# Other instruction times in a source-level scheduler, and a place reserved by Gram, in a delta-rule and SoLU kernel

## The chip, the cores and the metric

The kernel runs on one core of a Trainium2 chip. The metric is device time of one execution in microseconds (us); the median of several executions is given, and one execution has also been recorded by the hardware profiler.

## What is computed

First a delta-rule attention over 768 steps, for 4 batches and 8 heads of width 48, then a SoLU layer with layer norm on the 3072 rows of width 384 that come out.

```python
def _attn_ref(q, k, v, beta):
    k_n = k / (np.linalg.norm(k, axis=-1, keepdims=True) + 1e-06)
    state = zeros((B, H, D, D))
    for t in range(S):
        y[:, :, t] = q[:, :, t] @ state            # per batch and head
        v_old = state^T k_n[:, :, t]
        state += beta[:, :, t] * outer(k_n[:, :, t], v[:, :, t] - v_old)

def _moe_ref(x, w_in, w_out, g_ln):
    h = x @ w_in                                   # 384 -> 1024
    solu = h * softmax(h)
    ln = (solu - mean(solu)) / sqrt(var(solu) + 1e-06) * g_ln
    return ln @ w_out                              # 1024 -> 384
```

## The kernel before

**Tiling.** The 768 steps are cut into 12 chunks of 64. A unit is one chunk of one pair of batches (`bp`), with its 8 heads, so there are 24 units. Inside a chunk the recurrence is replaced by a triangular system. Its matrix is inverted for a whole group `m` of units at once: group 0 and group 6 hold two units, groups 1 to 5 four each (`units`, line 437).

**The steps of a unit.** `gram` (line 498) multiplies the keys with themselves (`gram`) and with the queries (`qk`), 16 pairs of products into two places of the PSUM pool `ps_f`; ScalarE copies the first to `g`, which SP stores to DRAM, and VectorE masks the second into `pm`, the tile that the text calls P, in a pool of ten places (line 503). `begin` (lines 806 to 812) loads the stored Grams of a group across partitions (`to_inv`), and prepares the matrix. `inversion` (line 799) runs 30 steps of two vector operations, `itmp` and `y`: on GpSimd (POOL) from group 2 on, shared between VectorE (DVE) and GpSimd for groups 0 and 1 (line 564). `inv_end` (line 577) stores the inverse (`zd`, `xd`) and loads it back transposed, in runs of 128 bytes, into `zt`, `gx` and `gy`. `tlevel` (line 639, in `block_level`) puts the blocks of the inverse together with small products (`mps`), which need both places of `ps_f`. `chain` (line 649) carries the state from unit to unit (`kps`, `ups`, `cps`, `yps`) and ends with two transposing DMAs of the unit's rows. `moe_h` (line 709) is the first layer (`h`, 18 products in one PSUM buffer), the softmax and the row sums on VectorE and ScalarE, and two more transposing DMAs; `moe_out` (line 759) is the second layer (`ops`, 24 products) and the store. At the start the weights arrive as 64-bit floats and `to_f32` (line 377) takes them apart with three bit operations on VectorE; the result is split in a high and a low fp16 part.

**What sets the order.** The source does not issue instructions as it runs. `Engine` and `Queue` wrap the engines and hand each call to a `Recorder` (line 117) with a duration in ns (`occ`) and a latency. `Engine` reckons `base + per * n` for n elements of a partition, with 150 + 1.04 n on VectorE, 110 + 0.96 n on ScalarE, 200 + 1.8 n on GpSimd and hand-set numbers for products (218 per product of the first layer, 165 of the second); a call with `accum_out` gets 190 more (line 282). `Queue` reckons 5 ns per KB of a DMA as time of the single queue SP, and 2000 ns more until the data are there (line 295). Each call also carries a rank (`prio`), which comes from its stream: unit i's chain is due at i - 1, its first layer at i + 1.15, its second at i + 2.5, the Grams of group m at 4m - 11 and later, its inversion from about 4m - 6.8 on (lines 832 to 854).

`Recorder.order` (line 178) then simulates the engines. Whenever one is free, it takes, of the calls whose inputs are there by its clock, the one with the lowest rank. A call that is the first to use a tile of a pool with few places can only go when a place is free, and is put back if not (lines 217 to 231). Products within `rec.atomic()` form one call. The result is one list of all calls in the order of their simulated starts. `emit` issues that list, and on the chip each engine runs its part of the list in order, waiting at each instruction for the semaphores of its inputs. The simulated times themselves are not used on the chip, only the order is.

`hold` (line 161) notes a use of a tile by the call added last, without an operand in the instruction. `order` then treats the tile as in use from that call on.

Of the kernel before, what the change touches and what calls it, by code (L numbers as in the profile page):

```python
# [11 lines left out]
ALU = mybir.AluOpType  # L12
# [4 lines left out]
P = 128  # L17
# [250 lines left out]
class Engine:  # L268


    def __init__(self, rec, name, real, base, per, lat):
        self.rec, self.name, self.engine, self.base, self.per, self.lat = rec, name, real, base, per, lat

    def __getattr__(self, op):
        fn = getattr(self.engine, op)

        def call(*args, n=None, ns=None, slack=0, **kw):
            if ns is None:
                if n is None:
                    v = kw["in_"] if op == "tensor_reduce" else kw["out"] if "out" in kw else args[0]  # L280
                    n = v.count()
                ns = self.base + self.per * n + (190 if "accum_out" in kw else 0)
            return self.rec.add(self.name, fn, args, kw, ns, self.lat, slack)

        return call


class Queue:
# [5 lines left out]
    def dma_start(self, kb, **kw):  # L294
        return self.rec.add(self.name, self.engine.dma_start, (), kw, kb * 5.0, 2000)

    def transpose(self, kb, **kw):
        return self.rec.add(self.name, self.engine.dma_start_transpose, (), kw, kb * 5.0, 2000)
# [7 lines left out]
def kernel(  # L306
# [26 lines left out]
    pe = Engine(rec, "PE", nc.tensor, 0, 0, 200)  # L333
# [43 lines left out]
    def to_f32(u, raw, scale, n, nm):  # L377
        if raw.dtype == F32:
            dve.tensor_scalar(out=u, in0=raw[:, :n], scalar1=scale, scalar2=None, op0=ALU.mult)
            return  # L380
        w = raw.bitcast(I32)
        lo, hi = w[:, 0 : 2 * n : 2], w[:, 1 : 2 * n : 2]
        c = p2.tile([P, 512], F32, tag="wc", name=f"wc_{nm}")[:, :n]
        act.activation(c, hi.bitcast(F32), AF.Square)
        gps.tensor_scalar(out=c, in0=c, scalar1=(1.125 * 2.0**-15) ** 2, scalar2=scale, op0=ALU.is_ge, op1=ALU.mult)
        f = u
        u = u.bitcast(I32)
        dve.tensor_scalar(out=u, in0=hi, scalar1=3, scalar2=0x3FFFFFF8, op0=ALU.logical_shift_left, op1=ALU.bitwise_and)
        dve.scalar_tensor_tensor(out=u, in0=lo, scalar=29, in1=u, op0=ALU.logical_shift_right, op1=ALU.bitwise_or)
        dve.scalar_tensor_tensor(out=u, in0=hi, scalar=-(1 << 30), in1=u, op0=ALU.bitwise_and, op1=ALU.bitwise_or)  # L390
        gps.tensor_tensor(out=f, in0=f, in1=c, op=ALU.mult)
# [106 lines left out]
    def gram(m, u, t0):  # L498
# [10 lines left out]
        for h2 in range(0, H, 2):  # L509
            with rec.atomic():  # L510
                for h, b2 in hb[2 * h2 : 2 * h2 + 4]:
# [7 lines left out]
                    )  # L519
        rec.after = None  # L520
# [11 lines left out]
    def to_inv(m):  # L532
        gi = p2.tile([P, 32, 32], F32, tag="ginv", name=f"ginv_{m}")
        ginv[m] = gi
        for b in range(4):
            blk = b % 2
            for z in range(1 if len(units(m)) == 4 else 2):
# [4 lines left out]
                    kb=128, out=gi[32 * b + 16 * z : 32 * b + 16 * z + n],  # L542
# [18 lines left out]
    def inv_step(m, j):  # L561
# [3 lines left out]
        for eng, c0, c1 in parts:  # L565
            if c1 <= c0:
# [8 lines left out]
            eng.tensor_tensor(out=y[:, c0:c1, j + 1 : 32], in0=y[:, c0:c1, j + 1 : 32], in1=tv, op=ALU.add)  # L575

    def inv_end(m):
# [13 lines left out]
        for b in range(4):  # L591
# [3 lines left out]
            sp.dma_start(kb=128, out=zz[rows, 0:n, blk * 32 : blk * 32 + 32], in_=zd[r0 : r0 + n].rearrange("l j i -> j l i"))  # L595
            if blk == 0:
                for t, r1 in ((xx, r0), (xy, r0 + 32)):
                    sp.dma_start(kb=128, out=t[r1 : r1 + 32, 0:n], in_=xd[r0 : r0 + n].rearrange("l j i -> j l i"))
            else:
                sp.dma_start(kb=128, out=xx[rows, 0:n], in_=src[rows, 0:n, 0:32])  # L600
# [108 lines left out]
    def moe_h(ch, bp, t0):  # L709
# [31 lines left out]
        dve.scalar_tensor_tensor(out=pl, in0=pr, scalar=sc, in1=ph, op0=ALU.mult, op1=ALU.subtract)  # L741
# [187 lines left out]
```

## Time and profile before

| | |
|---|---|
| median of 3 executions | 515.21 us (514.75 to 515.44) |
| the profiled execution | 512.04 us |
| its span, first to last instruction | 510.2 us |
| TensorE, matrix products | 368.2 us busy, 72% |
| VectorE | 318.6 us, 62% |
| GpSimd (POOL) | 294.0 us, 58% |
| ScalarE | 192.9 us, 38% |
| transfers of the queue SP | 70.8% of 16 DMA engines |
| granted clock of TensorE, mean | 0.92 |

Times in rows of the profile are microseconds from the start of the span unless marked ns. PE is TensorE, PEld its weight loads, DVE VectorE, ACT ScalarE, SP the engine that issues the DMAs. A group of instructions is named by the tile that it writes and those that it reads (`h<-win_hi,xth`), with shapes, count, busy time and the mean of one. All instructions bear line 265, since `emit` issues them all. What stands behind `<-` at the end of a row is what ended the idle time before the instruction. Products overlap, so their mean times add up to more than they take.

### The profile page before, as it was taken

Reading aid. Unit: us, or ns where it says so; the run is one execution under the profiler, and the core shown is the slowest. Engines: PE = TensorE matmul, PEld = TensorE weight load, DVE = VectorE, ACT = ScalarE, POOL = GpSimd, SP = SyncE. Lnnn points to the kernel's source line nnn. Section 1 sums busy time; section 2 is a strip of 40 time slices with the busy share of each in tenths; the row PEclk is TensorE's granted clock in tenths of the full one; section 3 lists DMA queues with packets and bytes.
Section 4 is the critical chain, followed back from the end, with each engine's and each line's share of the span. In section 5 each row is a group of like instructions: output and inputs, shape, how many; then the busy total and the mean of one; then the engine's idle time right before and its main releaser. Section 6 shows DMA issues by size and latency. Waiting matters only on the chain.

```text
span 510.2 us, 18246 instructions
## 1 busy us (share of the span) xinstructions
PE 368.2 (72%) x7744; PEld 233.9 (46%) x7744; DVE 318.6 (62%) x791; ACT 192.9 (38%) x382; POOL 294.0 (58%) x506
## 2 busy tenths in 40 slices
PE   3510070689579488997598997787969797899974
PEld 3410070455346345665366564444635464566532
DVE  3599999887884383655088664256597355455670
ACT  2210241465522143536144544224345345454450
POOL 3378385966558998984016886008989898100000
PEclk9999999877876699998799998898989899999998
DMA  8685662987989949977999587985656866744332
GB/s 212 159 255 98 155 169 65 161 171 174 172 162 165 179 113 160 168 135 161 189 165 144 145 162 151 160 162 95 107 118 144 145 114 128 131 64 99 73 68 61
DMA packets 180640, 72.21 MB, mean 142 GB/s; under 512 B 165520, under 2 KB 168976, under 8 KB 180560
## 3 DMA queue, kind: packets, MB, share of 16 engines
q1 hardware_dynamic: 180560, 71.06, 70.8%
q8 instruction: 60, 0.98, 0.9%
q14 instruction: 20, 0.16, 0.1%
HBM read 37.21 MB, written 16.52 MB: 105 GB/s over the span
## 4 chain that ended last, share of the span: by engine, by line
POOL 28%; PE 22%; DVE 19%; issue 10%; DMA 9%; SPq 7%; ACT 4%; POOLq 0%; DVEq 0%; ACTq 0%
POOL y L265 13%; POOL itmp L265 11%; PE h L265 7%; SPq L265 7%; PE ops L265 7%; DVE y L265 5%; DVE itmp L265 4%; DMA zt<-zd 3%; DMA ginv<-gd 3%; PE mps L265 2%; DVE wf L265 2%; DVE rst L265 1%; DVE st L265 1%; PE kps L265 1%; PE yps L265 1%
## 5 line engine op out<-in xcount | busy, mean ns | idle before, releaser
L265 POOL TENSOR_TENSOR y<-y,itmp 128x84 f32<-128x84 f32 (+16 forms) x190 | 100.7, 530 | 14.6
L265 POOL TENSOR_TENSOR itmp<-y,ginv 128x84 f32<-128x84 f32 (+16 forms) x190 | 93.3, 491 | 14.0
L265 DVE TENSOR_REDUCE st<-h 128x1 f32<-128x1024 f32 x24 | 29.3, 1222 | 87.5 <-PE h L265 82.2
L265 PE MATMUL qk<-kq 48*64 48x64 f32 x768 | 40.4, 269 | 24.9 <-DVE pm L265 15.6
L265 PE MATMUL gram<-kq 48*64 48x64 f32 x768 | 43.2, 270 | 18.8 <-DMA kq<-kq_dram 11.5
L265 POOL TENSOR_TENSOR st<-st,nhalf 128x1 f32<-128x1 f32 x24 | 13.2, 551 | 64.1 <-DVE st L265 64.1
L265 PEld LDWEIGHTS gram<-kq 48*64 48x64 f32 x768 | 37.5, 178 | 25.7 <-ACT g L265 6.3
L265 PEld LDWEIGHTS <-pth 128*128 128x128 f16 x384 | 37.6, 99 | 25.5 <-issue 1.7
L265 PE MATMUL h<-win_hi,xtl 128*128 128x512 f16 x144 | 45.4, 419 | 5.3 <-DVE pr L265 2.6
L265 PE MATMUL mps<-zt,gx 32*32 32x32 f32 x768 | 13.5, 205 | 48.6 <-issue 28.9
L265 PE MATMUL h<-win_lo,xth 128*128 128x512 f16 x144 | 46.7, 421 | 1.7 <-POOL win_lo L265 1.7
L265 PEld LDWEIGHTS qk<-kq 48*64 48x64 f32 x768 | 35.8, 178 | 25.3 <-DVE pm L265 16.1
L265 PEld LDWEIGHTS <-xth 128*128 128x128 f16 x288 | 28.4, 105 | 39.7 <-issue 14.8
L265 PE MATMUL ops<-wout_hi,ptl 128*128 128x384 f16 x192 | 38.7, 345 | 8.7 <-DMA ptl<-pl 6.8
L265 PE MATMUL h<-win_hi,xth 128*128 128x512 f16 x144 | 43.4, 411 | 0.0
L265 ACT ACTIVATE e<-h,st 128x1024 f32<-128x1024 f32 x24 | 26.7, 1114 | 38.0 <-DVE st L265 26.4
L265 POOL TENSOR_SCALAR_AFFINE_SELECT y<-y 128x1024 f32<-128x1024 f32 x7 | 9.4, 1346 | 53.5 <-DVE y L265 53.5
L265 DVE TENSOR_SCALAR st<-st 128x1 f32<-128x1 f32 (+1 forms) x216 | 35.5, 165 | 5.6
L265 PE MATMUL ops<-wout_lo,pth 128*128 128x384 f16 x192 | 36.9, 334 | 0.0
L265 PEld LDWEIGHTS mps<-zt,gx 32*32 32x32 f32 x768 | 10.1, 117 | 56.9 <-issue 34.8
L265 PE MATMUL ops<-wout_hi,pth 128*128 128x384 f16 x192 | 35.5, 326 | 0.0
L265 PE MATMUL cps<-u,kv 64*64 64x48 f32 x704 | 28.9, 235 | 9.1 <-ACT u L265 3.2
(94 smaller groups left out, 860.4 us busy)
## 6 DMA issues: line engine op xcount, KB each, us to landing
kq<-kq_dram SPq DMA_DIRECT2D x48, 192.0 KB, 4.5
kv<-kv_dram SPq DMA_DIRECT2D x24, 384.0 KB, 4.3
gd<-g SPq DMA_DIRECT2D x48, 128.0 KB, 3.3
out_dram<-oc SPq DMA_DIRECT2D x24, 192.0 KB, 2.2
zd<-y SPq DMA_DIRECT2D x7, 512.0 KB, 2.6
wi<-w_in_dram SPq DMA_DIRECT2D x6, 512.0 KB, 4.4
wo<-w_out_dram SPq DMA_DIRECT2D x8, 384.0 KB, 4.0
ginv<-gd SPq DMA_DIRECT2D x20, 128.0 KB, 4.2
```

What stands on the lines that cost most here:

```text
L265: fn(*[real(a) for a in args], **{k: real(a) for k, a in kw.items()})
```

## The change

The constants of the scheduler change, and `gram` reserves a place of P. No instruction is changed.

- A DMA is reckoned at the largest of 500 ns, 5 ns per KB, and 1.2 ns per contiguous run, where the number of runs is given: 1024 for the transposing loads of `inv_end` and, for a full group, those of `to_inv`. Until the data are there it takes 2300 ns more in place of 2000.
- All products are reckoned 1.06 times as long.
- The surcharge of 190 ns for `accum_out` goes.
- The three bit operations of `to_f32` are reckoned at 250 + 1.3 n.
- VectorE's operations in the shared steps of the inversion are reckoned at 230 + 1.04 per element.
- The residual `pl` of the epilogue is reckoned at 1420 ns.
- Each group of products in `gram` holds `pm`, so in the simulation the first of them takes the place of P, and waits for it.

```diff
-                ns = self.base + self.per * n + (190 if "accum_out" in kw else 0)
-            return self.rec.add(self.name, fn, args, kw, ns, self.lat, slack)
+                ns = self.base + self.per * n
+            return self.rec.add(self.name, fn, args, kw, ns * self.scale, self.lat, slack)
...
-    def dma_start(self, kb, **kw):
-        return self.rec.add(self.name, self.engine.dma_start, (), kw, kb * 5.0, 2000)
+    def dma_start(self, kb, runs=0, **kw):
+        return self.rec.add(self.name, self.engine.dma_start, (), kw, max(500.0, kb * 5.0, runs * 1.2), 2300)
 
     def transpose(self, kb, **kw):
-        return self.rec.add(self.name, self.engine.dma_start_transpose, (), kw, kb * 5.0, 2000)
+        return self.rec.add(self.name, self.engine.dma_start_transpose, (), kw, kb * 5.0, 2300)
...
-    pe = Engine(rec, "PE", nc.tensor, 0, 0, 200)
+    pe = Engine(rec, "PE", nc.tensor, 0, 0, 200, 1.06)
...
-        dve.tensor_scalar(out=u, in0=hi, scalar1=3, scalar2=0x3FFFFFF8, op0=ALU.logical_shift_left, op1=ALU.bitwise_and)
+        dve.tensor_scalar(ns=250 + 1.3 * n, out=u, in0=hi, scalar1=3, scalar2=0x3FFFFFF8, op0=ALU.logical_shift_left, op1=ALU.bitwise_and)
...
                         ns=60, out=pps[half(b2), h], lhsT=k[dims(b2), h, 0], rhs=k[dims(b2), h, 1],
                         start=True, stop=True,
                     )
+            rec.hold(pm)
...
-                    kb=128, out=gi[32 * b + 16 * z : 32 * b + 16 * z + n],
+                    kb=128, runs=32 * n, out=gi[32 * b + 16 * z : 32 * b + 16 * z + n],
...
+            ns = 230 + 1.04 * c * n if eng is dve else None
             eng.tensor_tensor(
-                out=tv, in0=y[:, c0:c1, j : j + 1].to_broadcast([P, c, n]),
+                ns=ns, out=tv, in0=y[:, c0:c1, j : j + 1].to_broadcast([P, c, n]),
...
-            sp.dma_start(kb=128, out=zz[rows, 0:n, blk * 32 : blk * 32 + 32], in_=zd[r0 : r0 + n].rearrange("l j i -> j l i"))
+            sp.dma_start(kb=128, runs=1024, out=zz[rows, 0:n, blk * 32 : blk * 32 + 32], in_=zd[r0 : r0 + n].rearrange("l j i -> j l i"))
...
-        dve.scalar_tensor_tensor(out=pl, in0=pr, scalar=sc, in1=ph, op0=ALU.mult, op1=ALU.subtract)
+        dve.scalar_tensor_tensor(ns=1420, out=pl, in0=pr, scalar=sc, in1=ph, op0=ALU.mult, op1=ALU.subtract)
```

The other bit operations, the second operation of a shared step and the other loads of `inv_end` are changed in the same way.

More of the change, by code (lines that the diff above doesn't have):

```diff
@@ L268, with __init__ @@
 class Engine:
-    def __init__(self, rec, name, real, base, per, lat):
-        self.rec, self.name, self.engine, self.base, self.per, self.lat = rec, name, real, base, per, lat
+    def __init__(self, rec, name, real, base, per, lat, scale=1.0):
+        self.rec, self.name, self.engine, self.base, self.per, self.lat, self.scale = rec, name, real, base, per, lat, scale
     def __getattr__(self, op):
@@ L387, in to_f32 @@
         u = u.bitcast(I32)
-        dve.tensor_scalar(out=u, in0=hi, scalar1=3, scalar2=0x3FFFFFF8, op0=ALU.logical_shift_left, op1=ALU.bitwise_and)
-        dve.scalar_tensor_tensor(out=u, in0=lo, scalar=29, in1=u, op0=ALU.logical_shift_right, op1=ALU.bitwise_or)
-        dve.scalar_tensor_tensor(out=u, in0=hi, scalar=-(1 << 30), in1=u, op0=ALU.bitwise_and, op1=ALU.bitwise_or)
+        dve.tensor_scalar(ns=250 + 1.3 * n, out=u, in0=hi, scalar1=3, scalar2=0x3FFFFFF8, op0=ALU.logical_shift_left, op1=ALU.bitwise_and)
+        dve.scalar_tensor_tensor(ns=250 + 1.3 * n, out=u, in0=lo, scalar=29, in1=u, op0=ALU.logical_shift_right, op1=ALU.bitwise_or)
+        dve.scalar_tensor_tensor(ns=250 + 1.3 * n, out=u, in0=hi, scalar=-(1 << 30), in1=u, op0=ALU.bitwise_and, op1=ALU.bitwise_or)
         gps.tensor_tensor(out=f, in0=f, in1=c, op=ALU.mult)
@@ L570, in inv_step @@
             tv = tmp[:, 0 : c * n].rearrange("p (c i) -> p c i", i=n)
+            ns = 230 + 1.04 * c * n if eng is dve else None
             eng.tensor_tensor(
-                out=tv, in0=y[:, c0:c1, j : j + 1].to_broadcast([P, c, n]),
+                ns=ns, out=tv, in0=y[:, c0:c1, j : j + 1].to_broadcast([P, c, n]),
                 in1=b[:, j : j + 1, j + 1 : 32].to_broadcast([P, c, n]), op=ALU.mult,
             )
-            eng.tensor_tensor(out=y[:, c0:c1, j + 1 : 32], in0=y[:, c0:c1, j + 1 : 32], in1=tv, op=ALU.add)
+            eng.tensor_tensor(ns=ns, out=y[:, c0:c1, j + 1 : 32], in0=y[:, c0:c1, j + 1 : 32], in1=tv, op=ALU.add)
     def inv_end(m):
@@ L594, in inv_end @@
             rows = slice(r0, r0 + 32)
-            sp.dma_start(kb=128, out=zz[rows, 0:n, blk * 32 : blk * 32 + 32], in_=zd[r0 : r0 + n].rearrange("l j i -> j l i"))
+            sp.dma_start(kb=128, runs=1024, out=zz[rows, 0:n, blk * 32 : blk * 32 + 32], in_=zd[r0 : r0 + n].rearrange("l j i -> j l i"))
             if blk == 0:
                 for t, r1 in ((xx, r0), (xy, r0 + 32)):
-                    sp.dma_start(kb=128, out=t[r1 : r1 + 32, 0:n], in_=xd[r0 : r0 + n].rearrange("l j i -> j l i"))
+                    sp.dma_start(kb=128, runs=1024, out=t[r1 : r1 + 32, 0:n], in_=xd[r0 : r0 + n].rearrange("l j i -> j l i"))
             else:
-                sp.dma_start(kb=128, out=xx[rows, 0:n], in_=src[rows, 0:n, 0:32])
+                sp.dma_start(kb=128, runs=1024, out=xx[rows, 0:n], in_=src[rows, 0:n, 0:32])
         ztx[m], gxt[m] = zz, (xx, xy)
```

## The prediction

> **What bounds the kernel now.** I read the page's span and its chain that ended last, then a table of stretches, and last the waits of TensorE.
>
> ```profile
> span 510.2 us, 18246 instructions
> ...
> POOL 28%; PE 22%; DVE 19%; issue 10%; DMA 9%; SPq 7%; ACT 4%; POOLq 0%; DVEq 0%; ACTq 0%
> ...
> 0.00:100.00 100.00, 30.67 (x839) 26.07 (x840) 79.31 (x195) 22.61 (x41) 61.49 (x113) 0.99 0.68 159
> 100.00:200.00 100.00, 77.08 (x1638) 48.46 (x1637) 69.53 (x156) 38.97 (x79) 75.38 (x109) 0.77 0.87 161
> 200.00:332.00 132.00, 113.17 (x2634) 71.81 (x2635) 70.00 (x178) 57.65 (x120) 72.15 (x131) 0.94 0.85 158
> 332.00:432.00 100.00, 84.60 (x1768) 51.19 (x1766) 61.24 (x159) 40.92 (x84) 78.13 (x139) 0.93 0.65 123
> 432.00:482.00 50.00, 44.93 (x776) 27.25 (x776) 26.87 (x72) 24.05 (x47) 5.34 (x13) 1.00 0.52 104
> 482.00:510.30 28.30, 17.79 (x90) 9.16 (x90) 11.62 (x33) 8.70 (x13) 1.48 (x4) 0.94 0.27 61
> ```
>
> In the table the columns are the stretch, its length, then busy time of PE, weight loads, DVE, ACT and POOL, the granted clock and the DMA share. Four regimes are to be seen. Up to 100 us the first two inversions and the decoding of the weights keep DVE busy for 79 of 100 us and TensorE waits. From 200 us on TensorE is busy 113.17 of 132 us, and again 44.93 of 50 before the tail: there, what TensorE waits for is what can be saved. From 332 to 432 us two inversions run back to back on POOL (78.13 of 100 us). The last 28 us are the epilogue of the last units and hold nothing that the change reaches except by its start. No single engine bounds the program, so a gain in one regime can be lost in the next.
>
> What TensorE waits for between 200 and 485 us, longest in total first:
>
> ```profile
> PE mps L265 <- DMA zt<-zd: 15.9, 5, 5.4
> ...
> PE h L265 <- DVE pr L265: 2.0, 1, 2.0
> PE ops L265 <- DMA ptl<-pl: 1.1, 1, 1.1
> ```
>
> 15.9 us in five waits have one cause: the first level product of a group of units, for which the loads of the inverse have not landed. They are these (the bracket is the idle time before):
>
> ```profile
> 201.59 0.34 PE L265 MATMUL mps<-zt,gx 32*32 32x32 f32 x17 [1.92 <-DMA zt<-zd]
> 250.75 0.64 PE L265 MATMUL mps<-zt,gx 32*32 32x32 f32 x30 [5.44 <-DMA zt<-zd]
> 324.67 0.45 PE L265 MATMUL mps<-zt,gx 32*32 32x32 f32 x30 [3.37 <-DMA zt<-zd]
> 400.00 0.38 PE L265 MATMUL mps<-zt,gx 32*32 32x32 f32 x23 [2.81 <-DMA zt<-zd]
> 447.16 0.33 PE L265 MATMUL mps<-zt,gx 32*32 32x32 f32 x16 [2.40 <-DMA zt<-zd]
> ```
>
> **What the change does to them.** Nothing that runs is added or removed: the same 18246 instructions, in another order on each engine. An engine runs its list in order, so a wait is an instruction that the source's scheduler put too early, since it reckoned with too short a way to it. The way to the level product of group 2 begins with the store of the inverse:
>
> ```profile
> 187.93 0.33 SPq L265 DMA_DIRECT2D zd<-y  x1
> ...
> 198.17 0.65 SPq L265 DMA_DIRECT2D zt<-zd  x1
> 198.93 1.30 SPq L265 DMA_TRANSPOSE ptl<-pl  x1
> ...
> zt<-zd SPq DMA_DIRECT2D x20, 128.0 KB, 4.2
> ```
>
> From that store to the product it took 201.59 - 187.93 = 13.7 us. The old constants make of it: the store 2.56 (512 x 5 ns), two of 0.64, eight strided loads of 0.64, an output of 0.96, and 2.0 to land: 11.9 us, so 1.8 short. The new ones charge a load of 1024 runs 1.23 us (1024 x 1.2 ns) and 2.3 to land: 2.56 + 1.28 + 8 x 1.23 + 0.96 + 2.3 = 16.9 us. That is 5.0 later than before, and 3.2 longer than it takes. Against this stands the factor 1.06 on matrix products. While an inversion runs on POOL, TensorE is busy some 86% (113.17 of 132), and the inversion of group 4 ran from 270.89 to 310.97:
>
> ```profile
> 270.89 1.26 POOL y L265
> ...
> 310.97 2.00 ACT ginv L265
> ```
>
> In these 40.1 us the scheduler's clock for TensorE now goes 40.1 x 0.86 x 0.06 = 2.1 us slower, while POOL's constants stay as they are, so the end of the inversion falls 2.1 us earlier in TensorE's list. The level product moves back by 5.0 - 2.1 = 2.9 us of other products. What is put in front exists: after the wait at 250.75 the rest of a first layer follows, after the one at 324.67 the rest of a second. So each wait shrinks by at most 2.9: 1.92 + 2.9 + 2.9 + 2.81 + 2.40 = **12.9 us gained**. If POOL's list also moved, all 15.9 could go, or, with the order as it is, nothing.
>
> A wait also has a follow-on that I leave out of the sum and keep for the range:
>
> ```profile
> 227.36 0.81 PE L265 MATMUL h<-win_hi,xth 128*128 128x512 f16 x3
> ...
> 252.15 1.49 PE L265 MATMUL h<-win_hi,xth 128*128 128x512 f16 x3
> ```
>
> Three products of the first layer took 0.81 us in a busy stretch and 1.49 us after the wait of 5.44. Over the stretch after that wait this was some 1.6 us, of the like after the one of 3.37; 0 to 3.2 us together. The Trainium skill (TensorE: Matmul & The Clock Gate, Part 1) says that the array falls to half its clock after an idle window of about 3.4 us and needs a busy one to come back. By that rule a wait of 5.44 cut to 2.5 would no longer trip the gate, and the forecast below would be 1.6 us lower.
>
> **The reserve of P.** One unit's Gram ran long before the place for its masked result was free:
>
> ```profile
> 169.88 0.31 PE L265 MATMUL qk<-kq 48*64 48x64 f32 x1
> 175.78 0.48 PE L265 MATMUL cs<-wout_lo,ones 128*128 128x384 f16 x1 [5.59 <-DVE wout_lo L265]
> ...
> 195.38 0.68 DVE L265 TENSOR_TENSOR pm<-qk,mask 128x512 f32<-128x512 f32 x1
> ...
> 304.70:305.90 1.20, 1.16 (x32) 1.02 (x32) 0.00 (x0) 1.00 1.07 149
> 167.80:170.30 2.50, 1.76 (x32) 1.47 (x32) 0.05 (x2) 0.81 1.22 167
> ```
>
> Its last product ended at 170.2, the mask came at 195.38, after the unit ten places earlier had been finished, and one of the two places of PSUM that level products need too was held for 25 us. With the reserve this Gram waits, unscheduled, until about 195. It leaves a stretch where TensorE then stood idle for 5.59 us and enters one where it is full. The last two rows are the Gram products of one unit alone, in a later full stretch and here: 1.16 us busy at full clock and 1.76 at the clock of 0.81. So **+1.2 us**, with bounds of 0, if the freed PSUM place lets a level product go earlier, and 1.8. Its stores come before the fourth inversion, which waits for later Grams anyway.
>
> **The other constants.**
>
> ```profile
> L265 DVE SCALAR_TENSOR_TENSOR wf<-wi,wf 128x512 int32<-128x512 int32 x12 | 12.0, 997 | 0.4
> L265 DVE TENSOR_TENSOR itmp<-y,ginv 128x210 f32<-128x210 f32 x2 | 0.9, 432 | 0.1
> L265 ACT ACTIVATE e<-h,st 128x1024 f32<-128x1024 f32 x24 | 26.7, 1114 | 38.0 <-DVE st L265 26.4 <-PE mps L265 11.5
> L265 ACT ACTIVATION_READ_ACCUMULATOR e<-h,st 128x1 f32 x24 | 4.7, 194 | 0.0
> L265 DVE SCALAR_TENSOR_TENSOR pr<-h,e 128x1024 f32<-128x1024 f32 x24 | 29.3, 1222 | 3.9 <-ACT e L265 3.3
> L265 DVE DVE_READ_ACCUMULATOR pr<-h,e 128x1 f32 x24 | 2.0, 83 | 0.0
> L265 DVE SCALAR_TENSOR_TENSOR pl<-pr,st,ph 128x1024 f16<-128x1024 f32 x24 | 32.3, 1345 | 2.6 <-ACT ph L265 2.0
> ```
>
> Bit operations go from 682 to 916 ns (997 measured), a shared step of 210 elements from 368 to 448 (432 measured). Both come nearer to the rows. They act in the first 180 us, where the rank of the work, and not its length, mostly settles who is next on a busy DVE: **0**, with bounds of 4 us either way, as four bit operations of 0.997 us may slip into the second inversion or out of it. The surcharge for running sums goes the wrong way. Exponential and product between them take 1114 + 194 + 1222 + 83 = 2613 ns; the scheduler had 1283 + 1405 = 2688 and now has 1093 + 1215 = 2308, so it believes the one buffer of the first layer free 0.30 us too early. The first layer itself is now reckoned 0.24 longer, which leaves 0.07 in each of 24 units: **+1.6 us**; bounds 0 and, without that cover, 24 x 0.30 = 7.3. The residual of the epilogue (1215 to 1420, 1345 measured) and 0.3 us more for every landing come nearer too, and there is little to win (1.1 us of waits on a transpose): 0.
>
> **The sum.** Of the gain, 2.81 + 2.9 fall at 400 and 324.67, next to a stretch that POOL's two inversions set; TensorE being early there helps half at best, so I take 2.9 back. -12.9 + 1.2 + 1.6 + 2.9 = -7.2 us. Durations are those of one profiled execution, of 512.04 us: 510.2 of span and 1.8 around it; it would come to 504.8. The median of the runs shown, 515.21, lies 3.2 above that execution; 515.21 - 7.2 = **508.0 us**.
>
> **The rivals.**
>
> *The end does not move* (514.2 to 516.2). The chain that ended last gives POOL the largest share, 28%. If the inversions' start at 344 us, and so their end at 431, comes out as it is, earlier waits are only exchanged for later ones. For it: from 332 us on the end follows POOL's 78 of 100 us. Against it: the products that start these inversions stand in the full stretch before 332, and 44.93 of 50 us before the tail are products, which any wait removed shortens. That the list hardly changes at all belongs here too.
>
> *The fifth inversion starts later* (slower). Its four loads stand behind other transfers in SP's list:
>
> ```profile
> 330.12 1.72 SPq L265 DMA_DIRECT2D out_dram<-oc  x1
> 331.90 2.63 SPq L265 DMA_DIRECT2D ginv<-gd  x4
> ...
> POOL y L265 <- DVE y L265: 29.6, 1, 29.6
> ```
>
> The last row, of the waits between 332 and 432 us, says that POOL had stood idle for 29.6 us before this inversion. By the constants a full group now costs the queue 4 + 10 strided loads x 0.59 = 8.3 us more, so that more work of better rank is ready each time the queue comes free. Two transposes of each kind (1.2 to 1.3 us, as in the row above) and a pair of loads of 0.5 each put ahead of row 331.90 make 6.0 us, and the path from there to the end is nearly all POOL: 515.21 + 6.0 = 521.2. It decides as soon as the added issues exceed the 7.2 gained elsewhere, or if that gain lies before 332 us and is swallowed. Against it: the same crowding would have to come at this place, and the inversion's loads rank before the later units' transposes.
>
> *The loads are overcharged* (slower). 16.9 us were reckoned against 13.7 taken. The landings of these loads spread widely:
>
> ```profile
> DMA to landing us min/median/max: 2.1/3.9/5.2
> ```
>
> If they came at the 2.1 end, the level products would stand 1.1 + 1.8 = 2.9 us behind their data, five times: 14.5 us, if there are only unready products in front. With the other terms: 515.21 - 12.9 + 14.5 + 5.7 = 522.5. The median of 3.9 and the five waits themselves speak against it. The Trainium skill (DMA: Bandwidth & Descriptors, Anatomy of one DMA) gives about 2 us plus bytes over 436 GB/s, for another issue path, which would be an estimated 2.3 us for 128 KB and speaks for this rival. The trace's median of 4.2 us for the full-size load does not agree with it.
>
> **How the numbers follow.** The forecast has 0.58, with its own range 500 to 513.5; an end that does not move 0.12; the later inversion 0.22; the overcharge 0.08. Below 0.2%, 1 us, a measurement of this kernel cannot tell a difference, so faster 0.58, same 0.12, slower 0.30. The range: downwards all five waits, their follow-on and a good start, 515.2 - 15.9 - 3.2 + 2 = 498; upwards the two slower rivals, to 523. I leave out 0.05 below, where the start wins its 4 us as well, and 0.08 above.
>
> **What would show it.** Right: waits of the level product on `zt<-zd` after 200 us sum to under 6 us instead of 15.9; the last load of a group's inverse has landed when TensorE comes to it; the Gram at 168 us stands near 195; the granted clock of 200 to 332 us rises from 0.94. Wrong: the same waits under another name (first layer on the product `pr`, chain products on POOL), which would refute the gain; POOL's start at 344 us later by more than 3 us, which would decide for the slower rival; a first stretch that ends more than 4 us off, which I have costed at nothing.

## The result, and the profile after

| | before | after |
|---|---|---|
| median of the executions | 515.04 us (514.75 to 515.44) | 530.94 us (528.74 to 535.71) |
| ratio, 95% interval | | 1.0321 [1.025, 1.0392] |
| profiled execution | 512.04 us | 531.36 us |
| its span | 510.2 us | 529.5 us |

The changed kernel is 3.2% slower. The forecast was 508.0 us, and 530.94 lies above the range of 498 to 523: the sign was wrong, and the rival that ended on this side was priced too low. Executions of two kernels below that took over 1.5% longer than the fastest of their kernel are left out of ratios and medians.

The page of the changed kernel, its span and the shares of the chain that ended last:

```profile
span 529.5 us, 18248 instructions
...
POOL 39%; PE 17%; issue 16%; DVE 15%; DMA 6%; SPq 3%; ACT 3%; POOLq 0%; DVEq 0%; ACTq 0%
```

POOL's share of the chain has grown from 28% to 39%, TensorE's has fallen from 22% to 17%: by this chain, the end now hangs more on the inversions than before. The table of stretches is cut at the places that answer to those of the kernel before: some 12 us ahead of the start of the fifth inversion, behind the sixth, and ahead of the epilogue (columns as in the prediction):

```profile
0.00:100.00 100.00, 27.22 (x770) 24.01 (x770) 76.58 (x190) 21.86 (x40) 59.48 (x113) 1.00 0.70 163
100.00:200.00 100.00, 75.55 (x1639) 49.73 (x1640) 68.47 (x157) 38.08 (x76) 73.92 (x100) 0.91 0.73 150
200.00:352.00 152.00, 120.98 (x2775) 76.20 (x2774) 72.51 (x184) 60.45 (x126) 76.02 (x141) 0.91 0.81 139
352.00:452.00 100.00, 83.33 (x1665) 52.86 (x1663) 62.02 (x156) 41.02 (x81) 78.99 (x139) 0.90 0.72 133
452.00:501.00 49.00, 45.84 (x811) 27.94 (x812) 29.01 (x78) 23.73 (x49) 4.52 (x12) 1.00 0.50 99
501.00:529.50 28.50, 18.52 (x89) 9.15 (x87) 10.52 (x29) 8.41 (x13) 1.48 (x4) 0.85 0.26 58
```

From the fifth inversion on, the stretches are as long as before (100, 49 and 28.5 us against 100, 50 and 28.3). The 20 us are in the third row, 152 us in place of 132, in which TensorE is busy 80% of the time and no longer 86%. (The first two rows are cut at the same times in both kernels, so what is lost in them shows up in the third as well.)

The waits of TensorE after 200 us, longest in total first (total, times, longest):

```profile
PE mps L265 <- ACT msb L265: 10.1, 3, 5.3
PE mps L265 <- DMA zt<-zd: 9.0, 3, 7.3
PE ups L265 <- DVE r L265: 6.9, 6, 5.2
PE yps L265 <- DVE xl L265: 5.7, 2, 3.3
PE h L265 <- DVE pr L265: 5.0, 3, 3.1
PE ups L265 <- DVE st L265: 3.4, 1, 3.4
```

The waits for the loads of the inverse have indeed fallen, from 15.9 us to 9.0, but the five other causes in this list sum to 31.1 us, where the kernel before had 7.9 for the same ones. All waits of TensorE together have risen from some 40 to some 51 us.

**The inversions one by one.** The trace gives, for the inversions that run on POOL alone, the start (POOL's selection `y<-y`, with which each begins) and the last operation `y`. All times in us; the last column is what lies between the end of the sixth and the end of the span.

| kernel | start 2 | 3 | 4 | 5 | 6 | end of 6 | to the end |
|---|---|---|---|---|---|---|---|
| before | 144.5 | 189.4 | 270.9 | 344.5 | 389.9 | 431.3 | 78.9 |
| after | 150.1 | 196.7 | 285.7 | 363.7 | 409.9 | 449.7 | 79.8 |
| difference | 5.6 | 7.3 | 14.8 | 19.2 | 20.0 | 18.4 | 0.9 |

So the loss has three places: 5.6 us ahead of the second inversion, 7.5 more ahead of the fourth, 4.4 more ahead of the fifth; steps of under 2 us between them are left aside. What follows the sixth takes as long as it did.

**Ahead of the fourth.** These are the DMAs that SP issues, the four loads of the Grams of group 4 in the kernel before:

```profile
253.64 3.85 SPq L265 DMA_DIRECT2D ginv<-gd  x4
```

and in the changed kernel:

```profile
263.19 0.93 SPq L265 DMA_DIRECT2D ginv<-gd  x2
267.63 1.20 SPq L265 DMA_TRANSPOSE xth<-xh  x1
268.88 0.57 SPq L265 DMA_DIRECT2D ginv<-gd  x1
269.75 1.63 SPq L265 DMA_TRANSPOSE pth<-ph  x1
271.48 1.21 SPq L265 DMA_TRANSPOSE xtl<-xl  x1
272.82 1.23 SPq L265 DMA_TRANSPOSE ptl<-pl  x1
274.16 1.33 SPq L265 DMA_DIRECT2D out_dram<-oc  x1
275.53 0.43 SPq L265 DMA_DIRECT2D ginv<-gd  x1
```

Four loads that stood together now have four transposes and a store between them, and the last goes out at 275.5. My reading is that a load reckoned at 1.23 us in place of 0.64 keeps the scheduler's queue occupied until other work of better rank is there; the experiments below test it.

**Ahead of the fifth.** The Gram loads of group 5 stand behind the inverse of group 4. On ScalarE and SP, in the kernel before:

```profile
310.97 1.99 ACT L265 COPY ginv<-y 128x1024 f32<-128x1024 f32 x1 [6.59 <-POOL y L265]
313.83 0.57 ACT L265 COPY g<-gram 128x512 f32<-128x512 f32 x1
...
310.96 0.36 SPq L265 DMA_DIRECT2D zd<-y  x1
321.31 1.40 SPq L265 DMA_DIRECT2D gd<-g  x2
```

The last Gram product of the group had started at 305.7. Its copy `g` waits on ScalarE behind the copy of an inverse that is not ready, its store `gd` on SP behind the inverse's stores and eight strided loads, and the loads that the next inversion needs come at 331.90, as the prediction showed. On SP of the changed kernel the order is the same, later, and two transposes more stand between the inverse's stores and its loads (330.35 and 331.65):

```profile
326.23 0.36 SPq L265 DMA_DIRECT2D zd<-y  x1
...
342.33 1.35 SPq L265 DMA_DIRECT2D gd<-g  x2
...
350.54 3.90 SPq L265 DMA_DIRECT2D ginv<-gd  x4
```

The selections with which the fourth and the fifth inversion begin, first in the kernel before and then in the changed one, with POOL's idle time ahead of each in the bracket:

```profile
270.88 1.26 POOL L265 TENSOR_SCALAR_AFFINE_SELECT y<-y 128x1024 f32<-128x1024 f32 x1 [4.95 <-DVE y L265]
...
344.46 1.26 POOL L265 TENSOR_SCALAR_AFFINE_SELECT y<-y 128x1024 f32<-128x1024 f32 x1 [29.61 <-DVE y L265]
```

```profile
285.67 1.26 POOL L265 TENSOR_SCALAR_AFFINE_SELECT y<-y 128x1024 f32<-128x1024 f32 x1 [37.85 <-DVE y L265]
...
363.68 2.25 POOL L265 TENSOR_SCALAR_AFFINE_SELECT y<-y 128x1024 f32<-128x1024 f32 x1 [20.80 <-DVE y L265]
```

**Ahead of the second.** The first product of the first layer, in the kernel before and in the changed one, and what stands ahead of it there:

```profile
94.01 0.49 PE L265 MATMUL h<-win_hi,xtl 128*128 128x512 f16 x1
```

```profile
110.73 0.48 PE L265 MATMUL cs<-wout_lo,ones 128*128 128x384 f16 x1 [6.26 <-DVE wout_lo L265]
...
122.52 1.46 PE L265 MATMUL h<-win_hi,xtl 128*128 128x512 f16 x3
```

The column sums of the output weights have moved ahead of the first layer, and TensorE waits 6.26 us at them for a weight that VectorE is still taking apart. Whether this is what delays the second inversion is tested below (`after_cs`).

### The profile page after: what moved, and what is told of

Read it like the earlier page. It is cut to its first block, busy times and chain, and to the rows that moved or that the text cites. A ratio compares the mean times of both kernels' runs of the same rounds, so it can differ in the third digit from the quotient of the medians.

```text
span 529.5 us, 18248 instructions
## 1 busy us (share of the span) xinstructions
PE 371.4 (70%) x7744; PEld 239.9 (45%) x7744; DVE 319.1 (60%) x791; ACT 193.6 (37%) x382; POOL 294.4 (56%) x506
## 4 chain that ended last, share of the span: by engine, by line
POOL 39%; PE 17%; issue 16%; DVE 15%; DMA 6%; SPq 3%; ACT 3%; POOLq 0%; DVEq 0%; ACTq 0%
POOL y L265 16%; POOL itmp L265 15%; PE h L265 5%; DVE y L265 4%; DVE itmp L265 4%; PE ops L265 4%; SPq L265 3%; POOL st L265 2%; POOL kv L265 2%; PE ups L265 2%; DVE wf L265 2%; PE mps L265 1%; DMA zt<-zd 1%; PE yps L265 1%; PE gram L265 1%
## 5 line engine op out<-in xcount | busy, mean ns | idle before, releaser
L265 POOL TENSOR_TENSOR itmp<-y,ginv 128x84 f32<-128x84 f32 (+16 forms) x190 | 95.8, 504 | 14.2
L265 POOL TENSOR_TENSOR y<-y,itmp 128x84 f32<-128x84 f32 (+16 forms) x190 | 95.3, 502 | 14.4
L265 PE MATMUL gram<-kq 48*64 48x64 f32 x768 | 44.5, 277 | 20.3 <-ACT g L265 9.7
L265 POOL TENSOR_TENSOR st<-st,nhalf 128x1 f32<-128x1 f32 x24 | 14.4, 602 | 77.5 <-DVE st L265 77.5
L265 PEld LDWEIGHTS gram<-kq 48*64 48x64 f32 x768 | 38.7, 185 | 27.0 <-ACT g L265 10.6
L265 PEld LDWEIGHTS qk<-kq 48*64 48x64 f32 x768 | 36.4, 185 | 19.5 <-DVE pm L265 10.2
L265 PE MATMUL yps<-u,pm 64*64 64x48 f32 x768 | 33.2, 244 | 11.2 <-DVE xl L265 8.0
L265 PE MATMUL ups<-r,zt 64*64 64x48 f32 x704 | 28.5, 237 | 11.4 <-DVE r L265 8.1
L265 DVE SCALAR_TENSOR_TENSOR pl<-pr,st,ph 128x1024 f16<-128x1024 f32 x24 | 31.6, 1318 | 7.9 <-ACT ph L265 7.5
```

What stands on the lines that cost most here:

```text
L265: fn(*[real(a) for a in args], **{k: real(a) for k, a in kw.items()})
```

## The experiments

Four theories were set against each other. **Queue**: the longer charge of the strided loads tears the Gram loads of a group apart. **TensorE**: the kernel is bound by its products from 200 us on, as the prediction had it. **Chain**: the end follows the inversions and what leads from one to the next. **Relative charges**: the scheduler reckons POOL's steps too short, so lengthening its other charges makes things worse. (The expectations call them Q, "my forecast", I and R; their V blames the remaining constants and the first 200 us.) Each kernel was measured beside the kernel before, and its ratio is to that.

### Which part of the change costs

`only_dma` is the kernel before with the DMA charges of the change alone, `without_dma` the changed kernel without them:

```diff
-        return self.rec.add(self.name, self.engine.dma_start, (), kw, kb * 5.0, 2000)
+        return self.rec.add(self.name, self.engine.dma_start, (), kw, max(500.0, kb * 5.0, runs * 1.2), 2300)
...
```

> The kernel before with the new transfer times alone. Theory Q (the queue: longer charges let other transfers in between the four loads of Gram that start an inversion, so that POOL starts later): in its order 4 transfers stand between the loads of group 4 and 19 between those of group 5, where before has none, so 10 to 25 us slower than before, 525 to 540 us. Theory V (the other constants make the loss, in the first 200 us): about as before, 513 to 518 us. My forecast before the result (the level products come later and their waits go) would give 500 to 510 us.

> The changed kernel with the old transfer times, all other edits in. Theory Q: no transfer between the loads of group 4 (4 between those of group 5), so most of the loss is gone: 512 to 521 us. Theory V: the loss stays, 526 to 533 us.

Measured: 531.79 us, 1.0323 [1.0284, 1.0361], and 532.97 us, 1.0345 [1.0295, 1.0396]. Each half of the change costs all of it: the first came out as Q had it, the second as V had it. Whatever one theory says of the DMA charge, it is not the only cause. `only_pe` has the factor 1.06 alone, `only_vec` the charges of the bit operations, the shared steps and `pl` alone:

```diff
-    pe = Engine(rec, "PE", nc.tensor, 0, 0, 200)
+    pe = Engine(rec, "PE", nc.tensor, 0, 0, 200, 1.06)
```

> The kernel before with the factor 1.06 on products alone; 4 transfers stand between the Gram loads of group 5. If the factor costs what stays without the new transfer times: 526 to 534 us. If it only shifts TensorE's list by the 2 us that my forecast reckoned, with a small loss by the split of group 5: 514 to 521 us.

> The kernel before with the new times of VectorE alone (bit operations, shared steps, residual). Its list puts the level products and Grams of group 1 ahead of the first layer. No transfer stands between the Gram loads of groups 4 and 5. Theory V (these constants cost the 3% that stays without the new transfer times): 526 to 534 us. If the factor on products or the reserve does that: 513 to 518 us.

Measured: 530.55 us, 1.0323 [1.029, 1.0356], and 521.21 us, 1.0126 [1.0088, 1.0164]. The first lies where it was expected if the factor costs it, the second between its two expectations. The parts do not add: 16.8, 15.9 and 6.6 us alone, 15.9 together.

### Moving single places of the list by hand

These kernels take the scheduler's list and move a few calls of it. `after_gi4` puts the four Gram loads of group 4 together again, behind the second of them in the list of SP, and `after_cs` puts the first two column-sum products back behind the first layer, ahead of the third (`label` gives the name of the tile that a call writes):

```diff
+    def together(ops, name):
+        sel = [o for o in ops if o.eng == "SP" and label(o) == name]
+        at = ops.index(sel[0])
+        ops[:] = [o for o in ops if o not in sel]
+        ops[at:at] = sel
+
+    together(done, "ginv_4")
```

```diff
+    sel = [o for o in done if label(o) == "cs"]
+    done = [o for o in done if o not in sel[:2]]
+    at = done.index(sel[2])
+    done[at:at] = sel[:2]
```

> The changed kernel, with only the third and fourth of the Gram loads of group 4 moved up in SP's list, behind the second; no other instruction changes its place. Theory Q: the last of these loads goes out near 264.5 us in place of 275.5, POOL's inversion of group 4 begins 9 to 11 us earlier (278 to 280 in place of 288.6), and the end follows by 7 to 11 us: 520 to 524 us. If the inversions are not what the end follows: within 3 us of the changed kernel, 528 to 534 us.

> The changed kernel, with only the first two of the products for the column sums moved back in TensorE's list, to before the third. Theory V in its narrow form (the level product of unit 2 stands behind a product that waits 6.3 us for the output weights): the first level product of group 1 goes from 111.1 to 104 to 106 us, the inversion of group 2 starts 4 to 6 us earlier, and the end follows by 3 to 6 us: 525 to 528 us. If the start of that inversion hangs on POOL or on the loads instead: no change, 529 to 533 us.

Measured: 524.57 us, 1.0191 [1.0143, 1.024], and 529.16 us, 1.0266 [1.0205, 1.0327]. The loads alone, 6.4 of the 15.9 us, just short of what theory Q had expected; the column sums 1.8, within the spread of the two kernels' executions. With the loads together, the fourth inversion begins at 277.4 in place of 285.7:

```profile
277.41 1.27 POOL L265 TENSOR_SCALAR_AFFINE_SELECT y<-y 128x1024 f32<-128x1024 f32 x1 [29.59 <-DVE y L265]
```

and the sixth ends at 440.7, 9.0 earlier, with 78.9 us behind it, as before. The queue theory holds for this place. `only_dma` splits the same four loads, `without_dma` does not. But the longer charge is not the only thing that splits loads: those of group 5 go out in two parts, 6.4 and 7.0 us apart, in `only_pe` and `without_dma`, which have the old DMA charges.

Moving the column sums did not bring the second inversion back. The first level product of group 1 ran at 103.4 us in place of 111.1, but the level products behind it then waited 8.85 us for ScalarE, and the inversion began at 149.4 in place of 150.1. So the wait at the column sums is not what delays it, and what does stays open.

`pe_copy` takes `only_pe` and moves the copy of the fourth group's inverse on ScalarE behind the next Gram's copy. The reason was this pair of rows of `only_pe`, first ScalarE, then TensorE:

```profile
316.50 1.94 ACT L265 COPY ginv<-y 128x1024 f32<-128x1024 f32 x1 [8.68 <-POOL y L265]
318.35 0.58 ACT L265 COPY g<-gram 128x512 f32<-128x512 f32 x1
...
318.98 0.36 PE L265 MATMUL gram<-kq 48*64 48x64 f32 x1 [7.65 <-ACT g L265]
```

ScalarE stands 8.68 us at the inverse; a Gram's copy is queued behind it, and TensorE waits 7.65 us for the place in PSUM.

```diff
+    copy = next(o for o in done if o.eng == "ACT" and label(o) == "ginv_4")
+    at = done.index(copy)
+    g = next(o for o in done[at:] if o.eng == "ACT" and label(o).startswith("g_"))
+    done.remove(copy)
+    done.insert(done.index(g) + 1, copy)
```

> The kernel with the factor 1.06 alone, with one instruction moved: ScalarE's copy at the end of the inversion of group 4 stands behind the copy of a Gram that stood right behind it. In that kernel ScalarE waits 8.7 us at this copy for POOL, the Gram copy comes late, and TensorE waits 7.6 us. Theory R (the factor makes the scheduler's POOL run ahead of its TensorE, so what needs the end of an inversion is put too early in the lists, and in-order engines pass the wait on): the wait of 7.6 us goes and the end follows by 4 to 8 us: 522 to 527 us. If that wait is covered by another: 528 to 532 us.

Measured: 530.65 us, 1.0335 [1.0302, 1.0368]: nothing gained. ScalarE alone was moved, the Gram's store and loads on SP were not. `before_gram_first` and `after_gram_first` therefore move the whole passage: the last Gram's copy ahead of the inverse's copy, its stores and the Gram loads of group 5 ahead of the inverse's stores, and the beginning of the fifth inversion earlier on VectorE, ScalarE and POOL (`pull` takes along what they need):

```diff
+    pull(min(at("ACT", "ginv_4"), at("SP", "zd_4")), lambda o: (o.eng, label(o)) == ("ACT", "g_10_1"))
+    pull(at("SP", "zd_4"), lambda o: (o.eng, label(o)) == ("SP", "ginv_5"))
+    first = [next(o for o in done if (o.eng, label(o)) == (e, "y_5")) for e in ("DVE", "POOL", "ACT")]
+    pull(at("DVE", "oc_5_0"), lambda o: o in first)
```

> The kernel before with one place of its list changed: the copy of the last Gram of group 5 stands ahead of the copy of the fourth group's inverse on ScalarE, its two stores and the four Gram loads ahead of the stores of that inverse on SP, and the beginning of inversion 5 correspondingly earlier on VectorE, POOL and ScalarE. Theory 'what stands behind the end of an inversion' (the Gram that the next inversion needs is queued behind the inverse): the fifth inversion starts at 326 to 333 us instead of 344.5, and the execution takes 500 to 509 us, although the inverse itself goes out about 5 us later. Rival 'the rest of the list is fixed': the start moves, but the end stays within 2 us, 512 to 517.

> The changed kernel with the same edit of its list. Here the Gram itself is ready only as the fourth inversion ends (its last product ends at 326 us), so the inverse goes out about 8 us later. Theory 'what stands behind the end of an inversion': the fifth inversion starts at 344 to 352 us instead of 363.7, the execution takes 513 to 524 us. Rival 'the rest of the list is fixed': the start moves, the end stays at 529 to 534.

Measured: 510.12 us, 0.992 [0.9889, 0.9951], and 526.29 us, 1.0235 [1.0189, 1.0282]: 4.2 and 4.7 us gained, between the two expectations of each. POOL of `before_gram_first` shows why:

```profile
328.44 1.26 POOL L265 TENSOR_SCALAR_AFFINE_SELECT y<-y 128x1024 f32<-128x1024 f32 x1 [11.48 <-DVE y L265]
387.26 1.27 POOL L265 TENSOR_SCALAR_AFFINE_SELECT y<-y 128x1024 f32<-128x1024 f32 x1 [12.92 <-DVE y L265]
```

The fifth inversion starts 16.1 us earlier, as the chain theory said. The sixth starts only 2.6 us earlier: where it had followed the fifth at once, POOL now idles 12.92 us, because the sixth's beginning stands where the list had it. A passage moved by hand wins what the next passage of the list allows.

### What the end follows

`before_less_pe` leaves out the products of the second layer with the low part of the output weights (8 of 24 in each unit), `before_short_inv` the steps 21 to 30 of the inversions of groups 2 to 6:

```diff
+    done = [o for o in done if not (label(o).startswith("ops_") and o.calls[0][2]["rhs"].root.name == "wout_lo")]
```

```diff
+            if m > 1 and j > 20:
+                steps.update(rec.ops[first:])
...
+    done = [o for o in done if not (o.eng == "POOL" and o in steps)]
```

> The kernel before, its order kept, without the pass of the second layer over the low part of the weights (8 of 24 products in each unit, so that part of the sum is left out). That is 8 x 0.167 = 1.34 us in each of 24 units, 32 us of TensorE. If the end follows what TensorE has to do from 200 us on, as my forecast assumed: 20 to 30 us faster, 485 to 495 us. Theory I (the end follows the chain of inversions on POOL, and products fill the time between): 0 to 9 us faster, 506 to 515 us, and the inversions begin where they did, within 3 us.

> The kernel before, its order kept, without the steps 21 to 30 of the inversions of groups 2 to 6 on POOL (the inverse is left incomplete). By the rows of these shapes that is 11 us less of POOL in each group, 56 us in all. Theory I: the end comes at least as much earlier as two to four groups, 22 to 45 us, 470 to 493 us. If TensorE's products set the end: at most the waits for the inverse, 16 us, go: 499 to 513 us.

Measured: 510.29 us, 0.9928 [0.9895, 0.9961], and 502.5 us, 0.9773 [0.9728, 0.9817]. The first is as theory I expected. The second misses its range and lies in that of its rival. TensorE was busy 368.2 us and is now 346.0: 22 us less work bring 4.4. That refutes the theory that the products bound the kernel from 200 us on. POOL's 294.0 us became 243.1; 51 us less bring 12.2, some 1.2 times what one of the five shortened inversions lost (51 / 5 = 10.2), where a plain chain of inversions would have brought nearly all of it. So the inversions are not the bound throughout either: between two of them lie Grams, stores and loads, whose place in the list stays. In `before_short_inv` the fourth inversion ends at 296.6 us, 14.3 earlier than in the kernel before, but the fifth starts only 5.5 earlier, and POOL idles longer ahead of it (35.56 us in place of 29.61):

```profile
338.93 1.27 POOL L265 TENSOR_SCALAR_AFFINE_SELECT y<-y 128x1024 f32<-128x1024 f32 x1 [35.56 <-DVE y L265]
```

### What the scheduler believes of POOL

The fourth inversion of the kernel before, its first and its last operation on POOL:

```profile
272.22 0.23 POOL L265 TENSOR_TENSOR itmp<-y,ginv 128x30 f32<-128x30 f32 x1
...
310.67 0.27 POOL L265 TENSOR_TENSOR y<-y,itmp 128x30 f32<-128x30 f32 x1
```

It takes 310.94 - 272.22 = 38.7 us. The scheduler reckons 60 operations of 200 + 1.8 n, with 9920 elements in all: 12.0 + 17.9 = 29.9 us, 8.8 short. In the trace the 60 operations are busy 32.8 us, and POOL idles 6.0 us in all in the short gaps between them. With 335 in place of 200 it reckons 38.0. `after_pool` is the changed kernel with this number, `after_pool_300` and `after_pool_370` have 300 and 370:

```diff
-            ns = 230 + 1.04 * c * n if eng is dve else None
+            ns = 230 + 1.04 * c * n if eng is dve else 335 + 1.8 * c * n
```

> The changed kernel with the longer POOL steps and nothing else. In its list no transfer stands between the Gram loads of any group. Theories Q and R together: the split and the early copies are gone, what is left is the start (3 us): 508 to 519 us. If neither is the cause: 526 to 533 us.

> The changed kernel with the steps of an inversion on POOL charged 300 + 1.8 n (after: 200 + 1.8 n, run at 335: 504.08 us). Theory 'relative charges' (the planner thought POOL too fast against the other engines): at 300 a group's 60 operations are charged 2.1 us less than at 335, so most of the gain stays, 501 to 511 us. Rival 'one lucky order' (335 happened to hit a good list): any place between 504 and 531 us, most likely above 515.

> The changed kernel with the steps on POOL charged 370 + 1.8 n, 2.1 us a group above what they take. Theory 'relative charges': too late is cheaper than too early, 502 to 511 us. Rival 'one lucky order': most likely above 515 us.

Measured: 504.08 us, 0.9823 [0.9786, 0.9861]; 508.37 us, 0.9876 [0.9824, 0.9927]; 503.64 us, 0.9794 [0.9747, 0.9841]. One number turns a loss of 3.2% into a gain of 1.2 to 2.1%, at three values, the first of them by more than was expected, so that one lucky list does not explain it. All three are faster than both kernels. The page of `after_pool`:

```profile
span 504.6 us, 18250 instructions
...
PE 26%; DVE 23%; POOL 17%; issue 16%; DMA 8%; ACT 5%; SPq 4%; POOLq 0%; DVEq 0%; ACTq 0%
```

POOL's share of the last chain is 17%, after 28% and 39%. Its SP around the end of the fourth inversion, at 322.2:

```profile
317.60 1.09 SPq L265 DMA_DIRECT2D gd<-g  x2
318.79 1.61 SPq L265 DMA_DIRECT2D kq<-kq_dram  x2
320.78 2.81 SPq L265 DMA_DIRECT2D ginv<-gd  x4
323.64 1.17 SPq L265 DMA_DIRECT2D zd<-y  x1
```

The Grams' stores and loads now go out ahead of the inverse, with no hand in the list: a scheduler that expects the inverse 8 us later finds the queue free for them. The fifth inversion starts 14.6 us after the end of the fourth, at 336.8 (33.5 after it in the kernel before, 37.5 in the changed one). The fourth starts at 282.1, 11.2 later than before, so the loss ahead of it has not gone: it is more than paid for here.

At this place the other charges matter little. In six kernels with the longer POOL charge (these three, and `hold_pool`, `ap_without_dma` and `ap_without_pe` below) the fifth inversion starts 4.2 to 20.9 us after the end of the fourth. In the six with POOL at 200 whose lists were not moved by hand (the kernel before, the changed one, `only_dma`, `without_dma`, `only_pe`, `only_vec`) it takes 33.5 to 41.4 us.

What each of the other charges is worth, once POOL's is right, say four more. `ap_without_dma` and `ap_without_pe` are `after_pool` without the DMA charges and without the factor; `hold_pool` is the kernel before with the reserve of P and 335 on POOL as the only new charge, `pe_hold_pool` the same with the factor (the reserve is in them because, without it, the longer POOL charge leaves no place for a tile in the scheduler's simulation).

```diff
+            rec.hold(pm)
...
+            ns = None if eng is dve else 335 + 1.8 * c * n
```

> The changed kernel with POOL at 335 + 1.8 n, and the DMA charges of before (5 ns per KB, 2000 ns to land). Theory 'relative charges': the strided loads are again reckoned too short, and level products stand before their loads have landed (up to 15.9 us of waits as in the kernel before): 506 to 518 us. Theory 'queue' (the longer charge costs by letting other transfers between the Gram loads of a group): this charge is gone, so faster than 504.08, 497 to 503 us.

> The changed kernel with POOL at 335 + 1.8 n, without the factor 1.06 on products. Theory 'relative charges': the factor did harm only because POOL was reckoned too fast beside it; with POOL at its own price it is worth little either way, 501 to 509 us. Rival 'the factor itself does harm' (it cost 15.9 us alone): taking it out gains again, below 499 us.

> The kernel before with the reserve of P and the same longer POOL steps, no other new constant. Theory R: the same waits (18.5 us before) shrink too, 500 to 513 us. If orders near the old one are only better or worse by accident: 513 to 530 us.

> The factor 1.06 and the reserve of P, with POOL's inversion steps charged 335 + 1.8 ns per element in place of 200 + 1.8 (38.0 us for a group in place of 29.9, which is what a group takes in the traces). Theory R: ScalarE's waits for POOL at the end of an inversion (20.4 us with the factor alone) halve, and most of the loss is gone: 510 to 521 us. If the loss comes from the factor whatever POOL is charged: 526 to 533 us.

The medians, in us, with the ratio to the kernel before:

| charges beside POOL's | POOL 200 + 1.8 n | POOL 335 + 1.8 n, P reserved |
|---|---|---|
| none of the new ones | 515.0 (before) | 523.47, 1.019 [1.0158, 1.0222] |
| factor 1.06 | 530.55, 1.0323 | 513.65, 0.9984 [0.9948, 1.002] |
| all but the DMA charges | 532.97, 1.0345 | 518.95, 1.0095 [1.006, 1.0129] |
| all but the factor | not run | 515.68, 1.0021 [0.9988, 1.0055] |
| all | 530.94, 1.0321 | 504.08, 0.9823 [0.9786, 0.9861] |

By itself, each new charge that was run costs (left column, and the runs above). With POOL at its price, the DMA charges on top of all others are worth 14 to 15 us and the factor 10 to 12, by the ratios and by the medians; on the left the DMA charges on top of the others bring 2.0, within the spread. Not every charge gains on the right: from the factor alone to all but the DMA charges the time rises by 5 us.

Expectations that missed: `hold_pool` was to gain by theory R and lost 1.9%. It lies in the range that its rival gave, lists that are better or worse by accident. Its trace says where it loses: the fourth inversion starts at 292.1 us in place of 270.9, 21 us later, and the fifth 14.7 us after the end of the fourth in place of 33.5, so that what is won behind the fourth is lost ahead of it. Whether POOL's charge or the reserve of P delays the fourth is not known. `ap_without_pe` came out above both of its expectations: the factor does no harm of its own there, and it is worth much more than I thought. `ap_without_dma` lies 1 us above its range. So POOL's charge settles the place behind the fourth inversion and turns the sign of the whole change; that right charges make a good list in general is not shown.

`ap_without_dma` shows what its expectation named, the old waits of the level products, of which `after_pool` has 0.5 us (TensorE from 200 to 485 us):

```profile
PE mps L265 <- DMA zt<-zd: 20.0, 5, 6.7
```

**What stays open.** The hand moves account for 6.4, 4.7 and perhaps 1.8 of the 15.9 us, each measured by itself; they were not tried together. Why the factor alone, without the queue's part, loses just as much was only read from rows such as those at 316.50, and moving that one copy did not help. It does not lose in the same places: in `only_pe` the sixth inversion ends 10.5 us later than in the kernel before, and 86.6 us follow it in place of 78.9, where the changed kernel loses only 0.9. And the charge of `accum_out` and the reserve of P were not run by themselves.

## Why the prediction was wrong

- **The bound.** "From 200 us on [...] what TensorE waits for is what can be saved" is the first step that failed. The five waits were real, and they did shrink, from 15.9 to 9.0 us where under 6 was forecast. But 22 us less work on TensorE brought 4.4 us, so a TensorE wait removed is not time gained, and other waits of TensorE grew by more than these shrank. The prediction had itself read that no engine bounds the program and that POOL has the largest share of the chain, and then added up TensorE's waits.
- **The sum of a wait, 5.0 - 2.1 = 2.9.** Both terms were right as charges. The step took everything else in the list as unmoved: SP's order above all, and POOL's starts. A charge that lengthens fourteen loads a group moves all that competes for SP, and the Gram loads were torn apart at 263 to 276 us. This place alone is worth 6.4 us.
- **The end of the inversion.** The rows at 270.89 and 310.97 stood in the prediction, 40.1 us with the selection at the head. I used them to find that the inversion's end moves 2.1 us earlier in TensorE's list, and did not set them beside the scheduler's own price of 29.9 us for the 60 steps. The scheduler already expected the inverse 8.8 us too soon, and the factor and the longer queue charges were corrections to the other side of an unbalanced pair. With POOL at 335, the same change is 1.8% faster than the kernel before, although 335 without the other new charges was no gain.
- **The rival that came true.** "The fifth inversion starts later" had the mechanism, its place and the row to watch, and 0.22. Its size was off: 6.0 us, where 19.2 were measured. It was worked out at one place, but the crowding came ahead of the fourth inversion (7.5 us), ahead of the fifth (4.4), and the start had lost 5.6 already. What spoke against it, that the inversion's loads rank ahead of the later units' transposes, is true of the rank and of no help: a rank counts only among calls that are ready when the queue comes free.
- **The start, costed at 0 with 4 us either way.** The second inversion starts 5.6 us later, and the vector charges alone cost 1.3%. "The rank of the work, and not its length, mostly settles who is next" was the failing sentence: the column sums went ahead of the first layer, which starts at 122.52 in place of 94.01. What holds the second inversion up is not known; moving the column sums back brought it 0.75 us.
- **The reserve of P.** The Gram at 168 us was to stand near 195. Its products now end at about 203, and the mask follows at once, as this row of VectorE shows; the price of the move, 1.2 us, was not measured by itself:

```profile
204.32 0.68 DVE L265 TENSOR_TENSOR pm<-qk,mask 128x512 f32<-128x512 f32 x1
```

- **The clock** of the third stretch was to rise from 0.94. It fell to 0.91. TensorE's load fell as well (80% in place of 86%), but no run shows that the one follows from the other.
- **The overcharge of the loads**, the rival with 0.08, did not come: TensorE still waited 9.0 us for such loads, so its products had not been put too far behind them, and with POOL priced right the same charge gains 14 to 15 us. The estimate of 2.3 us for such a load, which the prediction took from the Trainium skill (DMA: Bandwidth & Descriptors, Anatomy of one DMA), for another issue path, is not what these loads take: the median of the changed kernel's Gram loads (count, size, us to landing) is

```profile
ginv<-gd SPq DMA_DIRECT2D x20, 128.0 KB, 4.2
```

## What to carry to other kernels

In a source-level list scheduler the charges count only against each other: before one of them is corrected, compare the reckoned and the measured length of every long operation on the way from one stage to the next (here 29.9 against 38.7 us for an inversion), and correct them together. A wait that the profile shows on the busiest engine is a place to look, not a sum to collect; to see what the end follows, take work away from one engine and see how much of it comes back. And when the list of one queue changes, follow its other customers: 6.4 of the 15.9 us lost here were four loads that had stood together.

## What the runs showed of the hardware

**Fewer products, and the clock.** With a third of the second layer left out, `before_less_pe` had a lower granted clock than the kernel before from 200 us on (0.90, 0.88 and 0.96 in place of 0.95, 0.91 and 0.98, from 200 to 300, 300 to 400 and 400 to 480 us), but a higher one from 100 to 200 (0.83 in place of 0.77), where TensorE had less to do as well. The mean clock of its three executions was 0.879 to 0.909; that of the kernel before, measured beside it, 0.887 to 0.927. That less work lowers the clock is therefore not shown here.

**A long wait has a tail.** TensorE of the changed kernel around its longest wait for an inverse:

```profile
252.32 0.81 PE L265 MATMUL h<-win_hi,xth 128*128 128x512 f16 x3
...
261.49 0.65 PE L265 MATMUL mps<-zt,gx 32*32 32x32 f32 x30 [7.32 <-DMA zt<-zd]
...
262.89 1.49 PE L265 MATMUL h<-win_hi,xth 128*128 128x512 f16 x3
264.31 0.34 PE L265 MATMUL cps<-u,kv 64*64 64x48 f32 x1
...
264.88 0.22 PE L265 MATMUL cps<-u,kv 64*64 64x48 f32 x1
```

Three products of the first layer take 0.81 us ahead of the wait and 1.49 behind it, and the small products of the chain are back at their full rate (0.22 us each in place of 0.34) at 264.88, 3.4 us after the end of the wait. The granted clock from 261.49 to 264.88 is 0.50, and 1.00 right behind. At half the rate over 3.4 us, the follow-on of this wait is an estimated 1.7 us, which is the size that the prediction gave the one at 250.75. The Trainium skill (TensorE: Matmul & The Clock Gate, Part 1), with half the clock after an idle window of about 3.4 us, agrees with these rows; no run changed the length of the wait alone.
